# Pooled attention and a cosine-gated MLP on one core: another queue and another type for batch 0's loads

## The chip, the core and the metric

The kernel runs on one core of a Trainium2 chip. A core has a matrix engine (TensorE, "PE" in the profile, with its weight loads listed apart as "PEld"), a vector engine (VectorE, "DVE"), an activation engine (ScalarE, "ACT"), a general engine (GpSimd, "POOL") and SyncE ("SP"), which here only issues transfers. Sixteen DMA engines move data between the memory (HBM) and the on-chip memory (SBUF). Matrix products land in a small accumulator memory (PSUM) of eight banks; here they are three pairs (`banks`) and two single ones (`obanks`). An instruction waits at the head of its engine's queue until what it reads is there, and everything behind it on that engine waits with it.

The metric is the device time of one execution in microseconds (us); lower is better.

## The reference

Attention over keys and values that were averaged over groups of 8 positions, and then a two-layer network with the gate h · cos(h):

```python
B, H, S, D = 8, 8, 576, 64
k_p = k.reshape(B, H, 72, 8, D).mean(axis=3)
v_p = v.reshape(B, H, 72, 8, D).mean(axis=3)
attn = softmax(q @ k_p.T / sqrt(D))           # per batch and head, 576 x 72
x = (attn @ v_p), heads side by side          # 4608 tokens x 512
h = x @ w_in                                  # 512 -> 2048
out = (h * cos(h)) @ w_out                    # 2048 -> 512
```

All inputs and the output are fp32 in HBM; q, k and v are 9.4 MB each, the two weights 4.2 MB each.

## The kernel before

The 4608 tokens are cut into 9 tiles of 512. The loop over the tiles (t) does for each: the up projection into the eight pairs of hidden chunks (`up_mm`, L297), the gate (`up_g`: the cosine on ScalarE, L304, the product on VectorE, L307), and the down projection (`down_mm`, L310), between whose matmuls the attention of the next batch (b = t + 1) is woven by hand: `fill` holds pairs of "after so many matmuls" and "do this". The order of every engine's instructions is that of the program; nothing reorders them.

Batch 0 has nothing to be woven into. Its attention is the prologue, L334 to L423, and runs before the loop:

- `warm_up` (L392) issues matmuls on a constant tile, whose results nobody reads.
- q, k and v of one batch are staged in bf16 as `staged["q", 0]` and so on: 128 partitions, four pairs of heads (j = 0 to 3), 9 rows of 64 values each.
- `pool_k_mm` (L157) pools k by matmuls against a 0/1 matrix `groups`, which VectorE computes from iotas at the start (L361 to L365); `put_kk` (L132) copies the sums into `kk` in four copies. It is called for head pairs 0 and 1, and later for 2 and 3.
- `q_transpose_mm` (L192) transposes q by 18 matmuls against `identity`, in four groups, each followed by a copy into `qT` (L193).
- `scores` (L211, then an exponential on ScalarE, L218) works on one *unit*: 256 queries of four heads. Batch 0 has units 0 to 3 and a rest of 64 queries, which is done in the loop.
- `pool_v_mm` (L165) pools v by 18 matmuls of 256 columns into the two banks of a pair, and one VectorE copy (L167) puts the sums into `vz[0]`, whose other columns were filled with a constant before.
- `sums_first` (L266, then on ScalarE a logarithm, L270, and an exponential, L271) gives the inverse of a unit's softmax sums; `values_then` (L280) multiplies with v, and VectorE writes the product with the inverse into `xT` (L282), which the up projection reads. Units 0 and 1 give the first half of xT's four rows of chunks (ki 0 and 1), units 2 and 3 the second half. At the end of the prologue, the ki 0 and 1 part of the first two up projections is issued.

Batch 0's loads. The first half of k (head pairs 0 and 1) is loaded by SyncE in fp32 into the still unused `g_sb`, and ScalarE casts it into the staging tile (L342, L343). The others are casting transfers, fp32 in HBM to bf16 in SBUF, issued by GpSimd (`load_even`, L84): first half of q, second half of k, second half of q, all of v. Behind them on GpSimd's queue stand, in order: the identity (two instructions), w_in parts 0, 1 and 2 (`load_w_in`, L112), batch 1's k, the first half of its q, w_in part 3, the second half of its q, w_out part 0 (`load_w_out`, L117), batch 1's v, three fills of constant tiles, and w_out parts 1, 2 and 3. Eight casting transfers can be outstanding: from the ninth on, each issue waits until the one eight places before it has landed. In tile 0, the down projection goes through w_out's parts in order; part 1 is read from the ninth matmul on.

Of the kernel before, what the change touches and what calls it, by code (L numbers as in the profile page):

```python
# [9 lines left out]
FP32 = mybir.dt.float32  # L10
# [4 lines left out]
POOL = 8  # L15
# [4 lines left out]
def kernel(  # L20
# [42 lines left out]
    xT = wpool.tile([128, KCH, n_tokens], BF16, name="xT")  # L63
    g_sb = wpool.tile([128, FFCH, TILE], BF16, name="g_sb")
# [58 lines left out]
    half = (slice(0, 64), slice(64, 128))  # L123

    def v_part(b):
        return vz[b % 2][:, :, 0:4:3, :]

    def put_kk(b, ps, pj0, pj1, copy):
        dst = kk[b % 2].rearrange("p (j a) n -> p j a n", a=2)
        for a in range(2):  # L130
            for r in range(2):
                copy(out=dst[half[r], pj0:pj1, a, 0:Sp], in_=ps[half[a]])  # L132

    def pool_add(b, which):

# [14 lines left out]
    def pool_k_mm(b, bank, pj0, pj1):  # L150

        kb = staged["k", b]
        ps = bank[:, 0:(pj1 - pj0) * Sp].rearrange("p (j n) -> p j n", n=Sp)
        for pj in range(pj0, pj1):
            for t in range(ROW):
                for rows in half:
                    nc.tensor.matmul(ps[rows, pj - pj0, :], lhsT=kb[rows, pj, t, :], rhs=groups[rows, t, :],  # L157
                                     start=(t == 0), stop=(t == ROW - 1))
        return lambda copy: put_kk(b, ps, pj0, pj1, copy)

    def pool_v_mm(b, pair):
        vb = staged["v", b]
        for t in range(ROW):
            for hp, rows in enumerate(half):
                nc.tensor.matmul(pair[:Sp, hp, 0:KCH * D], lhsT=groups[rows, t, :], rhs=vb[rows, :, t, :],  # L165
                                 start=(t == 0), stop=(t == ROW - 1))
        nc.vector.tensor_copy(out=v_part(b).rearrange("p j a d -> p a j d"),  # L167
                              in_=pair[:Sp, :, 0:KCH * D].rearrange("p a (j d) -> p a j d", j=KCH))
# [31 lines left out]
    def scores(b, u, pair):  # L200
        scores_mm(b, u, pair)
        scores_exp(b, u, pair)
# [57 lines left out]
    def sums_first(b, u, cs):  # L260

        (c0, n), (h0, nh) = u
        ex = att["ex", b, u]
        for i in range(nh):
            hp = i % 2
            nc.tensor.matmul(cs[hp * 64:hp * 64 + 64, (i // 2) * n:(i // 2 + 1) * n], lhsT=ones[:Sp, :],  # L266
                             rhs=ex[:, ex_col(u, i):ex_col(u, i) + n])
        w = nh * n // 2
        lnc, inv = inverse_tile(w)
        nc.scalar.activation(out=lnc, in_=cs[:, 0:w], func=ACTF.Ln)  # L270
        nc.scalar.activation(out=inv, in_=lnc, func=ACTF.Exp, scale=-1.0)  # L271
        att["inv", b, u] = inv

    def values_then(b, u, ao):

        (c0, n), (h0, nh) = u
        ex = att.pop(("ex", b, u))
        for i in range(nh):
            pj, hp = divmod(h0 + i, 2)
            nc.tensor.matmul(ao[hp * 64:hp * 64 + 64, (i // 2) * n:(i // 2 + 1) * n],  # L280
                             lhsT=vz[b % 2][:, pj, 3 * hp, :], rhs=ex[:, ex_col(u, i):ex_col(u, i) + n])
        nc.vector.tensor_mul(out=x_out(b, u, slice(0, 128)), in0=cols(ao, u), in1=cols(att.pop(("inv", b, u)), u))  # L282
# [55 lines left out]

    kv_even_tiles(0)
    q_tile(0)  # L340
    k_first = g_sb.rearrange("p f n -> p (f n)").bitcast(FP32)[:, 0:2 * ROW * D]
    nc.sync.dma_start(out=k_first.rearrange("p (j n) -> p j n", j=2), in_=even_view(k, 0, 0, 2))  # L342
    nc.scalar.copy(out=staged["k", 0][:, 0:2].rearrange("p j t d -> p (j t d)"), in_=k_first)  # L343

    row_of = consts.tile([128, ROW], FP32, name="row_of")
    for rows in half:
# [2 lines left out]
    first_of = consts.tile([128, Sp], FP32, name="first_of")  # L349
    nc.gpsimd.iota(first_of, pattern=[[POOL, Sp]], base=0, channel_multiplier=0,  # L350
                   allow_small_or_imprecise_dtypes=True)
    load_even(staged["q", 0], 0, q, 0, 2)
    load_even(staged["k", 0], 0, k, 2, 4)
    load_even(staged["q", 0], 0, q, 2, 4)
    load_even(staged["v", 0], 0, v)
    identity = consts.tile([128, 128], BF16, name="identity")
    make_identity(nc, identity)
    dist = consts.tile([128, ROW, Sp], FP32, name="dist")
    sign = consts.tile([128, ROW, Sp], FP32, name="sign")
    groups = consts.tile([128, ROW, Sp], BF16, name="groups")  # L360
# [2 lines left out]
    nc.vector.scalar_tensor_tensor(out=sign, in0=dist, scalar=1.0 - POOL, in1=dist, op0=ADD,  # L363
                                   op1=mybir.AluOpType.mult)
    nc.vector.tensor_scalar(out=groups, in0=sign, scalar1=0.0, scalar2=None, op0=mybir.AluOpType.is_le)  # L365
    nc.vector.memset(vz[0], float(POOL))
    ones = consts.tile([128, D], BF16, name="ones")
    nc.vector.memset(ones, float(POOL))
    gate = consts.tile([1, 1], BF16, name="gate")
# [2 lines left out]

    kv_even_tiles(1)
    q_tile(1)
    for cg in range(3):
        load_w_in(cg)
    load_even(staged["k", 1], 1, k)
    load_even(staged["q", 1], 1, q, 0, 2)
# [1 line left out]
    load_even(staged["q", 1], 1, q, 2, 4)  # L380
    load_w_out(0)
    load_even(staged["v", 1], 1, v)
    nc.gpsimd.memset(vz[1], float(POOL))
    for i in range(2):
        nc.gpsimd.memset(kp2[i], 0.0)
    for cg in range(1, 4):
# [7 lines left out]
    vec, act = nc.vector.tensor_copy, nc.scalar.copy  # L394
    us = BY_HEADS

    warm_up(10, obanks[0])
    pool_k_mm(0, obanks[1], 0, 2)(vec)
    warm_up(2, banks[1][:, 0, :])
    puts = q_transpose_mm(0, banks[2][:, 0, :], 0, 5), q_transpose_mm(0, obanks[0], 5, 9)  # L400
    puts[0](vec)
    puts[1](act)
    warm_up(2, banks[1][:, 0, :])
    scores(0, us[0], banks[0])
    scores(0, us[1], banks[1])
    pool_k_mm(0, obanks[1], 2, 4)(vec)
    sums_first(0, us[0], banks[0][:, 0, :])
    for put in (q_transpose_mm(0, banks[2][:, 0, :], 9, 14), q_transpose_mm(0, obanks[0], 14, 18)):
        put(vec)
    sums_first(0, us[1], obanks[1])  # L410
    warm_up(2, banks[1][:, 0, :])
    scores(0, us[2], banks[0])
    scores(0, us[3], banks[2])
    pool_v_mm(0, banks[1])
    sums_first(0, us[2], obanks[0])
    values_then(0, us[0], obanks[1])
    values_then(0, us[1], banks[1][:, 0, :])
    sums_first(0, us[3], banks[2][:, 0, :])
# [6 lines left out]
    for t in range(NT):  # L425
        b = t + 1
# [108 lines left out]
```

## Time and profile before

| | us |
|---|---|
| runs | 302.17, 302.63, 302.64; median 302.63 |
| the profiled execution's span, first to last instruction | 301.4 |
| TensorE busy in the span | 293.9 (97%) |
| ScalarE, VectorE, GpSimd busy | 205.7, 170.8, 130.4 |
| first half of k (SyncE, fp32): issued, landed | 0.75, 4.4 |
| v of batch 0 (GpSimd, casting): issued, landed | 3.85, 14.5 |
| second pair of scores on TensorE | 13.07 to 13.70 |
| first up projection matmul (L297) | 18.38 |
| first down projection matmul (L310) | 34.62 |
| last matmul's end | 298 |

How to read it: the span is that of one execution that was recorded instruction by instruction; the runs' times also hold what lies before the first and behind the last instruction. "Busy" counts the time in which an engine worked on an instruction, its idle time is put down to what ended it. The chain of waits is followed back from the last instruction, at each step to what released it, so that its pieces add up to the span. A transfer's landing is the moment at which its completion is seen, reckoned from its issue. The table's times of single instructions are those of the timeline; its landings are issue plus "issue to landing" in the list of DMA issues, or the start of what waited for them.

### The profile page before, as it was taken

What the parts mean: (1) busy time and instruction counts of PE and PEld (TensorE: products, weight loads), DVE (VectorE), ACT (ScalarE), POOL (GpSimd) and SP (SyncE); (2) the same over time, 40 slices, a digit from 0 to 9 for tenths busy, and PEclk for the clock granted to TensorE, in tenths of its full rate; (3) what the DMA queues carried; (4) which work ended last, traced back from release to release, by engine and by line L of the source; (5) the groups of instructions that cost most, each with busy time, mean ns of one, the idle gap of its engine ahead of it and who ended that gap; (6) DMA issues with size and microseconds to landing.
All of it is one profiled execution on the core that took longest, in us unless ns stands there. A gap on an engine that the chain in (4) does not pass through costs nothing.

```text
span 301.4 us, 4625 instructions
## 1 busy us (share of the span) xinstructions
PE 293.9 (97%) x1816; PEld 143.2 (48%) x1816; DVE 170.8 (57%) x212; ACT 205.7 (68%) x254; POOL 130.4 (43%) x93
## 2 busy tenths in 40 slices
PE   8789999999999999999999999999999999999995
PEld 3445544445544454445444544455444544444444
DVE  5448637465467446754666556654775477425712
ACT  3786798469876987688778886789668966605500
POOL 8463016984983398239913990389300000000000
PEclk9999999999999999999999999999999999999999
DMA  7999999639526961697079617791811130131023
GB/s 152 197 207 206 206 205 195 141 55 176 117 60 124 167 127 29 146 158 140 6 170 143 129 36 171 94 174 39 141 32 35 37 70 0 37 70 35 0 67 75
DMA packets 44165, 32.91 MB, mean 109 GB/s; under 512 B 22128, under 2 KB 39408, under 8 KB 44144
## 3 DMA queue, kind: packets, MB, share of 16 engines
q0 software_dynamic: 19744, 18.07, 38.3%
q1 hardware_dynamic: 24160, 14.42, 20.5%
q8 instruction: 14, 0.23, 0.3%
q10 hardware_dynamic: 240, 0.13, 0.2%
q14 instruction: 7, 0.06, 0.1%
HBM read 36.70 MB, written 9.44 MB: 153 GB/s over the span
## 4 chain that ended last, share of the span: by engine, by line
PE 93%; DMA 4%; POOL 1%; DVE 1%; issue 0%; POOLq 0%; DVEq 0%
PE bank L297 41%; PE obank L310 41%; PE bank L241 5%; DMA kv_st<-in_v_dram 4%; PE bank L211 3%; PE bank L328 1%; PE bank L165 1%; POOL q_b L84 1%; PE obank L157 0%; PE obank L280 0%; PE obank L192 0%; DVE xT L282 0%; DVE vz L167 0%; POOL kv_st L84 0%; DVE o_sb L316 0%
## 5 line engine op out<-in xcount | busy, mean ns | idle before, releaser
L310 PE MATMUL obank<-w_out_sb,g_sb 128*128 128x512 bf16 x560 | 131.4, 379 | 0.0
L297 PE MATMUL bank<-xT,w_in_sb 128*128 128x512 bf16 x576 | 126.6, 379 | 0.0
L304 ACT ACTIVATE cos<-bank,half_pi 128x1024 f32<-128x1024 f32 x72 | 79.3, 1113 | 59.5 <-PE bank L297 59.5
L307 DVE TENSOR_TENSOR g_sb<-bank,cos 128x1024 bf16<-128x1024 f32 x72 | 87.3, 1223 | 43.0 <-ACT cos L304 42.9
L297 PEld LDWEIGHTS <-w_in_sb 128*128 128x128 bf16 x576 | 56.1, 98 | 67.6 <-issue 1.6
L310 PEld LDWEIGHTS <-g_sb 128*128 128x128 bf16 x560 | 52.8, 98 | 56.5 <-issue 2.0
L252 DVE TENSOR_TENSOR xT<-bank,inv 64x512 bf16<-64x512 f32 (+1 forms) x72 | 45.3, 629 | 40.8 <-ACT inv L248 40.1
L141 POOL TENSOR_TENSOR kv_st<-kv_st 72x2048 f32<-72x2048 bf16 x12 | 48.7, 4058 | 33.9 <-DMA kv_st<-in_k_dram 33.9
L247 ACT ACTIVATE lnc<-bank 64x512 f32<-64x512 f32 (+1 forms) x72 | 39.2, 544 | 3.1 <-PE bank L241 1.7
L316 DVE COPY o_sb<-obank 128x512 f32<-128x512 f32 x35 | 23.6, 689 | 30.9 <-PE obank L310 30.5
L218 ACT ACTIVATE ex<-bank 72x1024 bf16<-72x1024 f32 (+1 forms) x40 | 35.0, 929 | 8.5 <-PE bank L211 8.4
L142 POOL TENSOR_TENSOR kv_st<-kv_st 72x1024 f32<-72x1024 f32 x12 | 28.2, 2349 | 1.0
L248 ACT ACTIVATE inv<-lnc 128x512 f32<-128x512 f32 (+1 forms) x36 | 21.0, 583 | 1.1
L241 PE MATMUL bank<-ex,vz 72*128 72x256 bf16 (+1 forms) x176 | 20.0, 243 | 0.0
L241 PEld LDWEIGHTS <-vz 72*128 72x128 bf16 x176 | 13.6, 97 | 9.6 <-DVE xT L252 0.5
L145 POOL TENSOR_TENSOR kp<-kv_st 72x512 bf16<-72x512 f32 x12 | 14.9, 1263 | 0.5
L211 PE MATMUL bank<-qT,kk 64*72 64x256 bf16 (+1 forms) x192 | 13.2, 252 | 0.0
L211 PEld LDWEIGHTS <-kk 64*72 64x72 bf16 x192 | 7.4, 109 | 9.9 <-issue 7.2
L285 ACT ACT_TABLE_LOAD x9 | 11.5, 1283 | 0.9 <-PEq L519 0.7
L499 POOL COPY gate<-kk 1x1 bf16<-1x1 bf16 x5 | 0.9, 179 | 25.7 <-DMA kk<-kp 25.7
L288 ACT ACT_TABLE_LOAD x9 | 11.5, 1283 | 0.2
L103 POOL DMA_DIRECT2D kv_st<-in_v_dram x6 | 5.0, 841 | 8.8 <-PE bank L165 8.8
(55 smaller groups left out, 93.1 us busy)
## 6 DMA issues: line engine op xcount, KB each, us to landing
out_dram<-o_sb SPq DMA_DIRECT2D x70, 128.0 KB, 2.4
kv_st<-in_v_dram POOLq DMA_DIRECT2D x8, 576.0 KB, 13.7
kv_st<-in_k_dram POOLq DMA_DIRECT2D x7, 576.0 KB, 7.6
q_b<-in_q_dram POOLq DMA_DIRECT2D x6, 576.0 KB, 9.9
w_in_sb<-in_moe_w_in_dram POOLq DMA_DIRECT2D x4, 512.0 KB, 14.5
w_out_sb<-in_moe_w_out_dram POOLq DMA_DIRECT2D x4, 512.0 KB, 18.1
q_b<-in_q_dram POOLq DMA_DIRECT2D x4, 288.0 KB, 13.0
g_sb<-in_k_dram SPq DMA_DIRECT2D x1, 576.0 KB, 3.7
```

The source lines that it names most:

```text
L141: add(out=s, in0=x[:, :, 0:4, :], in1=x[:, :, 4:8, :], op=ADD)
L142: add(out=s[:, :, 0:2, :], in0=s[:, :, 0:2, :], in1=s[:, :, 2:4, :], op=ADD)
L211: nc.tensor.matmul(pair[:Sp, bank, c:c + n].rearrange("p (g n) -> p g n", n=64), lhsT=kk[b % 2][half[r], h0 + i, 0:Sp], rhs=att["qT", b][h ...
L218: nc.scalar.activation(out=ex[:, 0:nh * n].rearrange("p (a n) -> p a n", a=2), in_=pair[:Sp, :, 0:nh * n // 2], func=ACTF.Exp, scale=scale ...
L241: nc.tensor.matmul(pair[:, hp, (i // 2) * n:(i // 2 + 1) * n], lhsT=vz[b % 2][:, pj, 2 * hp:2 * hp + 2, :].rearrange("p a d -> p (a d)"), ...
L247: nc.scalar.activation(out=lnc[half[1 - hp]], in_=pair[half[1 - hp], hp, 0:w], func=ACTF.Ln)
L252: nc.vector.tensor_mul(out=x_out(b, u, half[hp]), in0=cols(pair[half[hp], hp, :], u), in1=cols(inv[half[1 - hp]], u))
L297: nc.tensor.matmul(h[:, j, :], lhsT=w_in_sb[fc // 4][:, ki, (fc % 4) * 128:(fc % 4 + 1) * 128], rhs=xT[:, ki, t * TILE:(t + 1) * TILE], st ...
L304: nc.scalar.activation(out=cos, in_=h, func=ACTF.Sin, bias=half_pi[:, :1])
L307: nc.vector.tensor_mul(out=g_sb[:, 2 * fp:2 * fp + 2, :], in0=h, in1=cos)
L310: nc.tensor.matmul(o, lhsT=g_sb[:, fc, ms * 128:(ms + 1) * 128], rhs=w_out_sb[fc // 4][:, fc % 4, :], start=(fc == 0), stop=(fc == FFCH - 1))
L316: nc.vector.tensor_copy(out=o[:, 0:n], in_=ps)
```

## The change

All of batch 0's q, k and v go over SyncE's queue in fp32, in six transfers of two head pairs each, in the order in which they are used: k, q, k, q, v, v. The first three land in `g_sb`, the other three in the last columns of `xT`, which later batches fill. Twelve casts (one head pair each, 128x576, `cast_first`) put them into the staging tiles in bf16: two on ScalarE, five on VectorE, five on GpSimd. GpSimd has no more loads of batch 0; its queue issues w_in part 0 behind its cast of v's first head pair, and the other loads behind its cast of v's last one. The constant fill of both `vz` moves to GpSimd's start. The prologue's own steps change as well: the last of the four first kk copies is ScalarE's, v is pooled and copied in two halves, with a cast between them on VectorE, the sums of units 2 and 3 follow the values of the units before them, and there are three fewer warm-up matmuls.

```diff
@@ put_kk @@
-                copy(out=dst[half[r], pj0:pj1, a, 0:Sp], in_=ps[half[a]])
+                put = copy[2 * a + r] if isinstance(copy, tuple) else copy
+                put(out=dst[half[r], pj0:pj1, a, 0:Sp], in_=ps[half[a]])
...
@@ pool_v_mm @@
-    def pool_v_mm(b, pair):
+    def pool_v_mm(b, pair, j0=0, j1=KCH):
         vb = staged["v", b]
+        n = (j1 - j0) * D
...
-                nc.tensor.matmul(pair[:Sp, hp, 0:KCH * D], lhsT=groups[rows, t, :], rhs=vb[rows, :, t, :],
+                nc.tensor.matmul(pair[:Sp, hp, 0:n], lhsT=groups[rows, t, :], rhs=vb[rows, j0:j1, t, :],
...
@@ the prologue @@
-    k_first = g_sb.rearrange("p f n -> p (f n)").bitcast(FP32)[:, 0:2 * ROW * D]
-    nc.sync.dma_start(out=k_first.rearrange("p (j n) -> p j n", j=2), in_=even_view(k, 0, 0, 2))
-    nc.scalar.copy(out=staged["k", 0][:, 0:2].rearrange("p j t d -> p (j t d)"), in_=k_first)
+    RAW = 2 * ROW * D
+    homes = [g_sb.rearrange("p f n -> p (f n)").bitcast(FP32)[:, i * RAW:(i + 1) * RAW] for i in range(3)]
+    homes += [xT[:, i, n_tokens - 2 * RAW:].bitcast(FP32) for i in range(3)]
+    raw = {}
+    for (w, src, j0), home in zip((("k", k, 0), ("q", q, 0), ("k", k, 2), ("q", q, 2), ("v", v, 0), ("v", v, 2)), homes):
+        raw[w, j0] = home.rearrange("p (j n) -> p j n", j=2)
+        nc.sync.dma_start(out=raw[w, j0], in_=even_view(src, 0, j0, j0 + 2))
+
+    def cast_first(w, j, copy):
+        copy(out=staged[w, 0][:, j].rearrange("p t d -> p (t d)"), in_=raw[w, j // 2 * 2][:, j % 2])
...
-    load_even(staged["q", 0], 0, q, 0, 2)
-    load_even(staged["k", 0], 0, k, 2, 4)
-    load_even(staged["q", 0], 0, q, 2, 4)
-    load_even(staged["v", 0], 0, v)
     identity = consts.tile([128, 128], BF16, name="identity")
     make_identity(nc, identity)
+    for i in range(2):
+        nc.gpsimd.memset(vz[i], float(POOL))
...
-    nc.vector.memset(vz[0], float(POOL))
...
-    for cg in range(3):
+    cast_first("k", 0, act)
+    cast_first("k", 1, vec)
+    cast_first("q", 0, pool)
+    cast_first("q", 1, act)
+    cast_first("k", 2, pool)
+    cast_first("q", 2, pool)
+    cast_first("v", 0, pool)
+    load_w_in(0)
+    cast_first("v", 3, pool)
+    for cg in range(1, 3):
         load_w_in(cg)
...
-    nc.gpsimd.memset(vz[1], float(POOL))
...
-    warm_up(10, obanks[0])
-    pool_k_mm(0, obanks[1], 0, 2)(vec)
-    warm_up(2, banks[1][:, 0, :])
+    warm_up(8, obanks[0])
+    pool_k_mm(0, obanks[1], 0, 2)((vec, vec, vec, act))
+    warm_up(1, banks[1][:, 0, :])
     puts = q_transpose_mm(0, banks[2][:, 0, :], 0, 5), q_transpose_mm(0, obanks[0], 5, 9)
     puts[0](vec)
     puts[1](act)
+    cast_first("k", 3, vec)
     warm_up(2, banks[1][:, 0, :])
     scores(0, us[0], banks[0])
     scores(0, us[1], banks[1])
+    cast_first("q", 3, vec)
     pool_k_mm(0, obanks[1], 2, 4)(vec)
...
     warm_up(2, banks[1][:, 0, :])
+    cast_first("v", 1, vec)
     scores(0, us[2], banks[0])
     scores(0, us[3], banks[2])
-    pool_v_mm(0, banks[1])
-    sums_first(0, us[2], obanks[0])
+    pool_v_mm(0, banks[1], 0, 2)
+    cast_first("v", 2, vec)
+    pool_v_mm(0, banks[1], 2, 4)
     values_then(0, us[0], obanks[1])
     values_then(0, us[1], banks[1][:, 0, :])
+    sums_first(0, us[2], obanks[0])
+    values_then(0, us[2], obanks[1])
     sums_first(0, us[3], banks[2][:, 0, :])
-    values_then(0, us[2], obanks[1])
     values_then(0, us[3], obanks[0])
```

More of the change, by code (lines that the diff above doesn't have):

```diff
@@ L159, in pool_k_mm @@
         return lambda copy: put_kk(b, ps, pj0, pj1, copy)
-    def pool_v_mm(b, pair):
+    def pool_v_mm(b, pair, j0=0, j1=KCH):
         vb = staged["v", b]
+        n = (j1 - j0) * D
         for t in range(ROW):
             for hp, rows in enumerate(half):
-                nc.tensor.matmul(pair[:Sp, hp, 0:KCH * D], lhsT=groups[rows, t, :], rhs=vb[rows, :, t, :],
+                nc.tensor.matmul(pair[:Sp, hp, 0:n], lhsT=groups[rows, t, :], rhs=vb[rows, j0:j1, t, :],
                                  start=(t == 0), stop=(t == ROW - 1))
-        nc.vector.tensor_copy(out=v_part(b).rearrange("p j a d -> p a j d"),
-                              in_=pair[:Sp, :, 0:KCH * D].rearrange("p a (j d) -> p a j d", j=KCH))
+        nc.vector.tensor_copy(out=v_part(b)[:, j0:j1].rearrange("p j a d -> p a j d"),
+                              in_=pair[:Sp, :, 0:n].rearrange("p a (j d) -> p a j d", d=D))
     def k_transpose(b):
@@ L374 @@
     q_tile(1)
-    for cg in range(3):
+    vec, act, pool = nc.vector.tensor_copy, nc.scalar.copy, nc.gpsimd.tensor_copy
+    cast_first("k", 0, act)
[8 more added lines that the diff above has]
+    for cg in range(1, 3):
         load_w_in(cg)
@@ L392, in warm_up @@
             nc.tensor.matmul(bank, lhsT=warm[:, 0:128], rhs=warm)
-    vec, act = nc.vector.tensor_copy, nc.scalar.copy
     us = BY_HEADS
-    warm_up(10, obanks[0])
-    pool_k_mm(0, obanks[1], 0, 2)(vec)
-    warm_up(2, banks[1][:, 0, :])
+    warm_up(8, obanks[0])
+    pool_k_mm(0, obanks[1], 0, 2)((vec, vec, vec, act))
+    warm_up(1, banks[1][:, 0, :])
     puts = q_transpose_mm(0, banks[2][:, 0, :], 0, 5), q_transpose_mm(0, obanks[0], 5, 9)
```

## The prediction

> **What bounds the kernel now.** First the busy shares on the page: TensorE is busy 97% of the span. So only TensorE's idle time can be won, and all of it lies in the first 18.4 us. Then the chain of waits in order of time, over the first 60 us:
>
> ```profile
> 3.85 10.62 DMA kv_st<-in_v_dram
> 14.51 0.72 PE bank L165 x10
> ...
> 15.78 0.70 DVE vz L167
> ...
> 17.04 0.70 DVE xT L282
> ...
> 17.78 0.63 PE obank L280 x8
> 18.41 8.80 PE bank L297 x40
> ```
>
> The load of batch 0's v is the wait that ends last. It lands at 14.5; L165 pools it, L167 copies it, L280 and L282 give xT, and at 18.4 the up projection (L297) starts. From there to the end the chain is TensorE alone: a shift that reaches this stage reaches the end in full.
>
> Next the DMA stretches. Columns: the stretch, its length, busy times by engine, clock, DMA share, GB/s.
>
> ```profile
> 3.00:3.50 0.50, 0.50 (x2) 0.15 (x1) 0.47 (x2) 0.00 (x0) 0.50 (x2) 1.00 1.04 410
> 14.00:43.00 29.00, 27.58 (x270) 14.68 (x270) 16.83 (x23) 23.59 (x33) 8.84 (x11) 1.00 1.23 206
> ```
>
> SyncE's one fp32 load runs at 410 GB/s. GpSimd's casting loads are counted in bf16: 206 GB/s written is 412 GB/s of fp32 read, so both kinds move the same data in the same time. And this stream never pauses from 5 to 43 us. How near TensorE runs to it is told by the issue of w_out part 1, the issue-to-landing time of that issue, and its first user:
>
> ```profile
> 20.69 0.75 POOL L117 DMA_DIRECT2D w_out_sb<-in_moe_w_out_dram  x1
> ```
> ```profile
> w_out_sb<-in_moe_w_out_dram POOLq DMA_DIRECT2D x1, 512.0 KB, 17.5
> ```
> ```profile
> 38.60 0.81 PE L310 MATMUL obank<-w_out_sb,g_sb 128*128 128x512 bf16 x3
> ```
>
> It lands at 20.69 + 17.5 = 38.2 and is read at 38.6: 0.4 us to spare. By the same sum, parts 2 and 3 land at 40.7 and 43.3 and are read at about 41.3 and 43.9 (0.6 each); w_in part 0 lands at 16.95, read at 18.4 (1.4); batch 1's v has 1.5, w_in part 3 1.7, the rest 1.9 or more. So there are two bounds: the chain through v, and 0.4 us behind it the weight stream. A gain above 0.4 us needs both to come earlier.
>
> **The change, step by step.** *Loads.* Six fp32 loads of 0.59 MB go out on SyncE from 0.75 on (0.46 us an issue, done by 3.6; its next work is at 46 us). k's first half lands at 4.4 as now; each further one costs 0.59/0.41 = 1.44: q 5.85, k 7.3, q 8.7, v 10.15, v 11.6. v's last half is 2.9 earlier than now.
>
> *Casts.* ACT: the row 128x1152 fp32 to bf16 takes 1.15, the 128x512 copy 0.59, so 576 columns about 0.66. VectorE: L365, fp32 to bf16 in SBUF, 0.50 for 648 columns, so 0.45 (bounds 0.36, half L361's two-input rate, and 0.75, all of it). GpSimd has no such row: a memset of 1024 columns takes 0.97, which gives 0.55; the two-input add L142 gives 2349/1024 x 576 = 1.3; the nearest, one input and two-byte output, is the affine select (128 columns, 0.29), so 0.7. All three are below the 1.44 spacing of the landings, so GpSimd keeps up.
>
> *Pass to the second scores.* k cast by ACT and VectorE 4.44-5.1 (now 5.6); pooling from 5.35 (now 5.85); four kk copies of 0.31 end 7.65 to 8.0 (now 8.46), one on ACT. q's transposes wait for GpSimd's cast (5.9-6.6) and end 7.6; qT copies end 8.2 and 8.6 (now 9.17, 9.49). The first scores move from 9.2 to 8.4, the exps to 9.1-11.0. Second pooling of k 9.2-10.0, kk copies to 11.3, qT to 12.1, second scores 12.2-12.8 (now 13.07-13.7): 0.9 won. VectorE's casts of k, q and v (0.45 each) lie in its gaps up to there; at 0.75 each they still do. Warm-ups fall from 16 to 13 and filled idle time; vz's fill (0.91, VectorE) goes to GpSimd, which is idle before 5.9.
>
> *v in halves.* Two poolings of 18 matmuls, paced by their weight loads (18 in 0.91), so 0.9 each where one took 1.17; two copies of 0.37 for one of 0.69. VectorE's cast of v's third part stands behind the first copy, and TensorE's second pooling behind that cast: 12.8-13.7 pool, 13.8-14.2 copy, 14.2-14.65 cast, 14.7-15.65 pool, to 16.15 copy. Values of units 0 and 1 then end at 16.05 and 16.55, their xT at 16.85 and 17.5: the up projection's first data is 0.8 earlier than now (18.32). But the sums of units 2 and 3 now follow the values. ACT, free at 15.35, starts L270 for unit 2 only at 16.95 (now 16.11); four activations of 0.63 follow, and unit 3's xT ends at 20.25 (now 19.6). TensorE starts L297 after the last values at 18.1, runs 8 matmuls (1.75) to 19.85 and waits for unit 3 until 20.3; now it is there at 20.15. So on this chain: +0.15, bounds -0.5 and +0.9 (the casts' ends; one more hop between engines at each of the six hand-overs, 0.06 each).
>
> *The weight stream.* w_in part 0 now stands behind GpSimd's cast of v: issue at 10.15 + 0.05 + 0.7 = 10.9 (bounds 10.6, 11.8), now 5.15. What an issue on an empty stream costs is seen at 94.83 us, where batch 4's loads are issued:
>
> ```profile
> 94.50:96.00 1.50, 1.50 (x9) 0.69 (x7) 1.00 (x2) 0.89 (x2) 1.35 (x3) 1.00 0.00 0
> 96.00:96.50 0.50, 0.50 (x4) 0.20 (x2) 0.50 (x1) 0.50 (x1) 0.50 (x2) 1.00 0.84 21
> 96.50:97.00 0.50, 0.50 (x4) 0.21 (x3) 0.03 (x1) 0.50 (x1) 0.50 (x1) 1.00 0.54 32
> 97.00:97.50 0.50, 0.50 (x4) 0.27 (x3) 0.47 (x1) 0.00 (x0) 0.28 (x1) 1.00 0.53 61
> 97.50:98.00 0.50, 0.50 (x4) 0.21 (x3) 0.50 (x1) 0.39 (x1) 0.00 (x0) 1.00 0.81 119
> 98.00:98.50 0.50, 0.50 (x5) 0.20 (x3) 0.25 (x1) 0.50 (x1) 0.00 (x0) 1.00 0.90 150
> ```
>
> Nothing flows for 1.3 us and the ramp loses (185+174+145+87+56)/206 x 0.5 = 1.57 from 96.0: the stream counts as full from 2.75 us after the issue (2.8 at 64.70; 3.3 for the first one, at 1.42; low bound 1.3, no ramp). So 13.65, while SyncE's data end near 11: the DMA engines idle 2.7 us, which they do not now. From part 0 to w_out part 1 there are 4 x 0.524 + 3 x 0.59 + 2 x 0.524 = 4.92 MB, 23.9 us at 206; a landing trails the bytes moved by 0.35 to 0.43 MB now, 1.9 us. Sum: 13.65 + 23.9 + 1.9 = 39.45, 1.25 after now's 38.2. Bounds: issue 10.6 + 1.3 gives -0.5, issue 11.8 + 3.3 gives +2.7. w_in part 0 lands near 17.7, before it is needed; the slacks of 1.4 and more also hold. At w_out part 1, TensorE arrives at 38.75 and waits 0.7.
>
> **Sum.** 0.15 + 0.7 = +0.85. The profiled span is 301.4, 1.2 below the runs' median of 302.63; that rest does not change. Predicted: 302.63 + 0.85 = 303.5.
>
> The Trainium skill (DMA: Bandwidth & Descriptors, Specifications) puts the HBM limit of one core at about 358 GB/s. No row here agrees: 410 for SyncE's load, 412 for the casting stream; by its figure each load would take 1.65, v's first half would land 0.8 later, and the sum, an estimate, would be +1.7.
>
> **The rivals.** (A) The forecast: a wait at w_out part 1 takes the place of the wait for v. For it: the 0.4 us, and two ramps alike. Against: the ramps seen are of 72-partition loads.
> (B) The ramp hides. With w_in part 0 on 128 partitions the stream is full soon after its first bytes, at 12.5; w_out part 1 lands at 38.3 and only the chain counts: +0.15, 302.8.
> (C) Faster: v early decides. If the stream is full by 11.9 (low bound), w_out part 1 lands 0.5 earlier, and if unit 3's xT comes by 19.3, which needs the 0.9 won at the second scores to pass through the late sums, TensorE gains 0.9: 301.7. Decides: w_out part 1 before 37.7. Against: GpSimd's issue behind the cast.
> (D) VectorE's casts hold GpSimd. v's two casts (12.1, 14.2) fall on GpSimd's cast and its issues of w_in 1 and after. If each holds it 0.45, and its own casts take 1.3 and not 0.7, the stream is 1.2 to 1.5 later still: about 304.8. For: GpSimd's issue beside L361 took 0.88, others 0.70. The Trainium skill (SBUF — State Buffer, SBUF: two separate sides) says that a VectorE fp32 copy within SBUF shuts GpSimd out, descriptors too; no run here shows it yet.
>
> **How the numbers follow.** About 0.2% (0.6 us) is what a measurement of this kernel can tell from no change. A 0.5, spread over +0.3 to +1.5: 0.43 slower, 0.07 same. B 0.25, same. C 0.09, faster. D 0.16, slower. Together faster 0.09, same 0.32, slower 0.59. The range takes A, B and most of D, and from C's side the chain's low bound: 302.2 to 305.0; the forecast's own is 302.9 to 304.2.
>
> **What would show it.** v's pooling starting near 12.8; w_in part 0 issued near 10.9, its bytes from 12.2; DMA idle around 12; w_out part 1 landing near 39.5 with TensorE waiting before it; unit 3's xT near 20.2. Wrong if w_out part 1 lands before 38.6, or if the up projection waits for w_in part 0.

## The result: slower, at the place that was named and by three times as much

| | before | changed |
|---|---|---|
| median of the runs, us (lowest to highest, 4 runs each) | 302.63 (302.17–302.75) | 305.24 (304.51–306.22) |
| ratio of the runs, 95% interval | | 1.0096 [1.0078, 1.0113] |
| span of the profiled execution | 301.4 | 304.0 (the longest; the others 302.4, 302.9, 303.3) |
| time outside the span (before: in its later executions, 1.73 to 1.86) | 1.8 | 2.15 |
| v of batch 0 seen as landed | 14.5 | 11.17 (first half) |
| w_in part 0 issued | 5.15 | 11.84 |
| first up projection matmul | 18.38 | 17.67 |
| w_out part 1 landed, first read | 38.2, 38.60 | 41.2, 41.23 |

The time rose by 2.6 us (0.96%) where +0.85 was forecast; 305.24 lies above the upper end of the range, 305.0. Ratios, here and below, are of fast executions alone; the one slow execution (308.23, over 1.5% above the fastest of its kernel, a later version) is left out of its ratio.

First the chain of waits of the changed kernel, 0 to 60 us, which answers to the chain shown of before. Columns: start, length, what.

```profile
2.77 8.40 DMA xT<-in_v_dram
11.17 0.05 issue
11.23 0.67 POOL kv_st L352
11.89 0.89 POOL w_in_sb L112
12.78 0.72 POOL kv_st L352
13.50 8.63 DMA w_in_sb<-in_moe_w_in_dram
22.13 0.29 issue
22.41 18.77 DMA w_out_sb<-in_moe_w_out_dram
41.19 0.04 issue
41.23 0.81 PE obank L312 x3
```

Before, the chain left the loads at 14.5 and was TensorE alone from 18.4 on. Now it stays with transfers up to 41.2: v lands, GpSimd casts it (L352), only then issues w_in part 0 (L112), casts again, issues the rest, and the weights arrive late one after the other. The line of w_out part 1's first reader on TensorE's timeline ends with the idle time ahead of it:

```profile
41.23 0.81 PE L312 MATMUL obank<-w_out_sb,g_sb 128*128 128x512 bf16 x3 [1.42 <-DMA w_out_sb<-in_moe_w_out_dram]
```

It starts 2.63 later than before's 38.60, the next tile's up projection 2.62 later (56.78 for 54.16 in the chains), and the last matmul ends 2.6 later: all of the span's loss arises ahead of this line. Span minus the start of this reader is 262.8 in both profiles (301.4 − 38.60, 304.0 − 41.23).

Then the stretches of half a microsecond (stretch, length, busy times by engine, clock, DMA share, GB/s), and the one of 14 to 43 that was shown of before:

```profile
10.50:11.00 0.50, 0.23 (x4) 0.23 (x5) 0.47 (x3) 0.50 (x1) 0.22 (x1) 1.00 1.04 397
...
12.50:13.00 0.50, 0.50 (x9) 0.29 (x8) 0.50 (x1) 0.47 (x2) 0.50 (x2) 1.00 0.00 0
13.00:13.50 0.50, 0.47 (x16) 0.41 (x16) 0.04 (x1) 0.50 (x2) 0.50 (x1) 1.00 0.02 4
13.50:14.00 0.50, 0.28 (x12) 0.13 (x6) 0.08 (x1) 0.50 (x1) 0.50 (x2) 1.00 0.70 45
14.00:14.50 0.50, 0.00 (x0) 0.00 (x0) 0.50 (x2) 0.50 (x2) 0.50 (x2) 1.00 0.81 104
14.50:15.00 0.50, 0.24 (x8) 0.24 (x10) 0.21 (x1) 0.50 (x1) 0.50 (x1) 1.00 1.12 172
15.00:15.50 0.50, 0.50 (x20) 0.41 (x16) 0.00 (x0) 0.13 (x1) 0.50 (x2) 1.00 1.22 201
...
17.00:17.50 0.50, 0.48 (x10) 0.26 (x6) 0.23 (x1) 0.47 (x2) 0.50 (x2) 1.00 0.92 96
17.50:18.00 0.50, 0.50 (x5) 0.21 (x3) 0.00 (x0) 0.47 (x2) 0.50 (x2) 1.00 0.82 102
...
20.00:20.50 0.50, 0.49 (x3) 0.25 (x3) 0.00 (x0) 0.50 (x1) 0.50 (x2) 1.00 1.23 201
```
```profile
14.00:43.00 29.00, 25.08 (x251) 13.07 (x255) 17.24 (x24) 20.25 (x28) 11.96 (x16) 1.00 1.19 195
```

SyncE's data end at 11.1, the weights' first bytes come at 13.5, and the rate climbs to 201 by 15.0. Then it falls to about 100 once more (16.5 to 18) and is full for good only from 20: two ramps where the prediction had one. Before, the stretch of 14 to 43 had 206 GB/s in the mean; now it has 195, and starts behind a gap.

### The profile page after: what moved, and what is told of

It is laid out like the page before. It is cut to its first block, busy times and chain, and to the rows that moved or that the text cites. A ratio compares the mean times of both kernels' runs of the same rounds, so it can differ in the third digit from the quotient of the medians.

```text
span 304.0 us, 4642 instructions
## 1 busy us (share of the span) xinstructions
PE 291.4 (96%) x1798; PEld 142.3 (47%) x1831; DVE 173.1 (57%) x216; ACT 206.3 (68%) x256; POOL 133.0 (44%) x95
## 4 chain that ended last, share of the span: by engine, by line
PE 84%; DMA 12%; issue 1%; POOL 1%; ACT 1%; SPq 1%; DVE 0%
PE obank L312 39%; PE bank L299 36%; DMA w_out_sb<-in_moe_w_out_dram 6%; PE bank L243 5%; PE bank L213 3%; DMA w_in_sb<-in_moe_w_in_dram 3%; DMA xT<-in_v_dram 3%; PE bank L330 1%; ACT ex L220 1%; SPq L349 1%; POOL kv_st L352 0%; POOL w_in_sb L112 0%; DVE o_sb L318 0%
## 5 line engine op out<-in xcount | busy, mean ns | idle before, releaser
L312 PE MATMUL obank<-w_out_sb,g_sb 128*128 128x512 bf16 x542 | 129.0, 380 | 2.3 <-DMA w_out_sb<-in_moe_w_out_dram 1.4
L243 PEld LDWEIGHTS <-vz 72*128 72x128 bf16 x176 | 13.6, 97 | 9.6 <-DVE xT L254 0.5
```

What stands on the lines that cost most here:

```text
L243: nc.tensor.matmul(pair[:, hp, (i // 2) * n:(i // 2 + 1) * n], lhsT=vz[b % 2][:, pj, 2 * hp:2 * hp + 2, :].rearrange("p a d -> p (a d)"), ...
L312: nc.tensor.matmul(o, lhsT=g_sb[:, fc, ms * 128:(ms + 1) * 128], rhs=w_out_sb[fc // 4][:, fc % 4, :], start=(fc == 0), stop=(fc == FFCH - 1))
```

## The experiments

Each is the changed kernel with one edit, unless it says "before". A ratio is to executions of before taken beside the run; their medians were 302.11 to 302.31, with median spans of 300.3 to 300.5. Time outside the span is a run's time less its span.

### Is it the late stream?

**Before with the stream made late.** Nothing of the change but its late weights: a copy of one element on GpSimd, which waits for v, stands ahead of w_in's issues.

```diff
     q_tile(1)
+    landed = consts.tile([1, 1], BF16, name="landed")
+    nc.gpsimd.tensor_copy(out=landed, in_=staged["v", 0][0:1, 0, 0, 0:1])
     for cg in range(3):
         load_w_in(cg)
```

> The kernel before with one thing added: a one-element GpSimd copy of staged v of batch 0 ahead of the weights' issues, so that w_in part 0 is issued when v has landed (14.5 us instead of 5.15). No other part of the change is in it. Theory 1: the DMA engines run empty after v; the stream counts as full at 14.5 + 2.75 = 17.3 and w_out part 1 lands at 17.3 + 25.8 = 43.1, 4.9 later than before; TensorE also waits for w_in part 0, near 20.5. The end is 4 to 5 us later than before's, about 307. Rival (the late start is hidden by later slack, and the changed kernel's loss comes from its casts and sums): within 1 us of before, or no more than the 2 us that the wait for w_in part 0 costs.

Measured: 305.92 (305.44–306.21), ratio 1.0122 [1.0104, 1.014]; spans 303.6 to 304.4. From its chain of waits:

```profile
3.83 9.74 DMA kv_st<-in_v_dram
...
13.81 2.18 POOL w_in_sb L112 x3
...
22.99 18.48 DMA w_out_sb<-in_moe_w_out_dram
```

The late stream alone, with none of the casts and none of the reordering, costs 3.8, and at the same reader (41.51). Three of the four executions had a mean granted clock of 0.994 or below; the one at full clock has a span of 303.6. In the profile the half clock (18.7 to 22.1) lies ahead of the reader, which waits for its weights all the same. The cost is below the 4 to 5 expected for two reasons: v landed at 13.6 here, not at 14.5 as in the profile of before, so that w_in was issued 0.9 earlier than reckoned; and the stream, with its three issues in a row, was full 2.3 after the first of them and not 2.75 (13.76; its shortfall below 206 GB/s from 14.5 to 20 sums to 1.54).

**The issues moved ahead of GpSimd's casts.** w_in parts 0, 1 and 2 go out behind its casts of k, q and v's first part; v's last cast follows.

```diff
     cast_first("k", 2, pool)
+    load_w_in(0)
     cast_first("q", 2, pool)
+    load_w_in(1)
     cast_first("v", 0, pool)
-    load_w_in(0)
+    load_w_in(2)
     cast_first("v", 3, pool)
-    for cg in range(1, 3):
-        load_w_in(cg)
```

> The changed kernel with one thing moved: GpSimd issues w_in parts 0, 1 and 2 between its casts (behind the casts of k's third head pair, q's third and v's first) and not behind the cast of v's first head pair. Theory 1 (the weight stream starts too late, and the wait at w_out part 1 sets the end): part 0 is issued near 9.3 us, its bytes flow when SyncE's end near 11, w_out part 1 lands near 37.9 instead of 41.2, TensorE doesn't wait for it, and the span falls by 2.3 from the changed kernel's, to about 301.3 to 301.6. Rival (the prologue's own chain sets the end: casts, late sums of units 2 and 3): the end doesn't move by more than 0.3. In between would say that the loads of q and v are slowed by the weights beside them.

Measured: 303.74 (302.78–306.02), ratio 1.0056 [1.0031, 1.0082]. The profiled span is 300.9; its timeline shows w_in part 0's issue and w_out part 1's reader:

```profile
8.46 0.95 POOL L112 DMA_DIRECT2D w_in_sb<-in_moe_w_in_dram  x1
```
```profile
38.04 0.81 PE L312 MATMUL obank<-w_out_sb,g_sb 128*128 128x512 bf16 x3
```

The issue is 3.4 earlier, and no idle time stands at the reader any more. Spans at full granted clock are 300.6 to 301.2, against 302.4 to 304.0 of the changed kernel and 299.8 to 301.0 of before beside it. So the order of GpSimd's queue is the cause of most of the span's loss: the middle of the four spans at full clock is 300.85, the changed kernel's 303.1, before's 300.4. The median shows less of it: four of the eight executions had a mean granted clock of 0.994 or below, with spans of 302.0 (one 303.9); see the third group.

**One load fewer.** w_in part 3 isn't loaded; part 2 is used in its place, so 0.52 MB less stand ahead of w_out part 1.

```diff
+    w_in_sb[3] = w_in_sb[2]
...
-    load_w_in(3)
```

> The changed kernel without the load of w_in part 3; its hidden chunks are computed with part 2, so the output differs from the reference's. The stream before w_out part 1 is 0.52 MB shorter, 2.55 us at 206 GB/s; nothing else changes. Theory 1: w_out part 1 lands near 38.6, the wait of 1.4 us before it and that of 0.3 for w_in part 3 go, and the span falls by 1.7 to 2.3. Rival (the chain of the prologue): no change.

Measured: 303.73 (303.09–304.26), ratio 1.0043 [1.0025, 1.0061]; spans at full clock 300.9 to 301.3 (three of six executions; the others, at 0.994, 301.9 to 302.1). TensorE comes to the reader, L313 here, without a wait:

```profile
39.27 0.81 PE L313 MATMUL obank<-w_out_sb,g_sb 128*128 128x512 bf16 x3
```

This profile is one of the 0.994. The casts, their order and their waits are the changed kernel's; only 2.5 us of transfer (0.52 MB at 206 GB/s) are gone, and with them 2.0 of the 2.7 that the changed kernel's spans lie above before's. So about 0.7 is left for anything else on TensorE's path.

**The sums back ahead of the values.** Unit 2's sums between the two poolings of v, unit 3's behind the second, as near to the order before as the halves allow.

```diff
     pool_v_mm(0, banks[1], 0, 2)
+    sums_first(0, us[2], obanks[0])
     cast_first("v", 2, vec)
     pool_v_mm(0, banks[1], 2, 4)
+    sums_first(0, us[3], banks[2][:, 0, :])
     values_then(0, us[0], obanks[1])
     values_then(0, us[1], banks[1][:, 0, :])
-    sums_first(0, us[2], obanks[0])
     values_then(0, us[2], obanks[1])
-    sums_first(0, us[3], banks[2][:, 0, :])
     values_then(0, us[3], obanks[0])
```

> The changed kernel with the sums of unit 2 between the two poolings of v and those of unit 3 behind the second one, ahead of the values; the loads stay late. Theory 1: unit 3's xT comes near 18.9 instead of 19.95, TensorE no longer waits for it in the up projection (0.4 us), and all of that is given back at w_out part 1: the time is the changed kernel's within 0.3 us. Rival (the prologue's chain sets the end): 0.6 to 0.8 us faster than the changed kernel.

Measured: 305.5 (304.19–305.86), ratio 1.0102 [1.0075, 1.0129]: the changed kernel's time. TensorE no longer waits for unit 3's xT. It waits for w_in's parts instead (0.49 and 0.50) and at the same reader as long as before the edit:

```profile
40.90 0.81 PE L312 MATMUL obank<-w_out_sb,g_sb 128*128 128x512 bf16 x3 [1.40 <-DMA w_out_sb<-in_moe_w_out_dram]
```

With the stream late, the order of the sums is worth nothing.

### Where does the second fall come from?

**All three issues in a row**, v's last cast behind them. It tells whether the fall at 16.5 comes from the cast that stands between the issues of parts 0 and 1.

```diff
-    load_w_in(0)
-    cast_first("v", 3, pool)
-    for cg in range(1, 3):
+    for cg in range(3):
         load_w_in(cg)
+    cast_first("v", 3, pool)
```

> The changed kernel with GpSimd's cast of v's last head pair moved behind the issues of w_in parts 1 and 2, so that the three issues stand together as they do in the run where v's landing alone held them back. Theory 1a (the second fall of the stream, 96 to 158 GB/s between 16.5 and 19.5 us, comes from the 1.66 us between the first and the second issue: a second ramp): the fall goes, w_out part 1 lands near 40.1 instead of 41.2 and the span falls by 0.8 to 1.1; the second pooling of v waits for its last cast, issued 1.5 later, near 15.0 and costs 0.2 at most. Rival 1b (the fall comes from VectorE's copies and products at that time, or from the ring's start as such): no change in landing beyond 0.3, the time is the changed kernel's.

Measured: 305.52 (304.96–306.43), ratio 1.0111 [1.0088, 1.0134]. From its stretches of 1 us:

```profile
14.00:15.00 1.00, 0.12 (x5) 0.23 (x7) 0.31 (x1) 1.00 (x2) 1.00 (x2) 1.00 1.20 197
15.00:16.00 1.00, 0.91 (x22) 0.66 (x20) 0.39 (x1) 0.24 (x1) 1.00 (x2) 1.00 1.25 208
16.00:17.00 1.00, 0.85 (x11) 0.64 (x12) 0.98 (x3) 0.18 (x1) 1.00 (x3) 0.78 1.22 198
17.00:18.00 1.00, 1.00 (x12) 0.83 (x8) 0.34 (x1) 0.97 (x2) 1.00 (x2) 0.50 1.25 209
18.00:19.00 1.00, 1.00 (x6) 0.28 (x3) 0.69 (x1) 0.94 (x3) 1.00 (x2) 0.50 1.24 206
...
23.00:24.00 1.00, 1.00 (x5) 0.38 (x4) 0.00 (x0) 0.44 (x1) 0.14 (x1) 0.81 1.21 209
```

The fall is gone (197 to 209 throughout), and w_out part 1 lands at 39.1 (issued 20.94, 18.2 to landing), 2 earlier; 1.8 earlier than in the changed kernel's second profile below, where part 0 was issued at the same time (11.41, here 11.43). So the cast between the issues made it. The time didn't follow: v's last cast ended at 14.8 and TensorE idled 1.5 ahead of the second pooling (busy 0.12 of 14 to 15), and then the column ahead of the DMA share, the granted clock, reads 0.50. By the shares at both ends (0.78 in 16 to 17, 0.81 in 23 to 24) the half clock lasted from 16.6 to 23.4. TensorE came to the reader at 40.99, now by its own slowness. That is one of the two executions at 0.988; the other two, at 0.998, have spans of 302.8 and 302.9, and what sets these no profile shows.

**First loads in two halves each**, nine SyncE loads instead of six, to see whether smaller loads are seen as landed sooner.

```diff
-        nc.sync.dma_start(out=raw[w, j0], in_=even_view(src, 0, j0, j0 + 2))
+        for j in ((0, 1), (1, 2)) if (w, j0) in (("k", 0), ("q", 0), ("v", 0)) else ((0, 2),):
+            nc.sync.dma_start(out=raw[w, j0][:, j[0]:j[1]], in_=even_view(src, 0, j0 + j[0], j0 + j[1]))
```

> The changed kernel with three of SyncE's six loads (first halves of k, q and v) cut in two: nine loads, the same bytes. Theory 2 (a landing trails the bytes moved by about one transfer, 0.59 MB, which is why v's first half lands at 11.2 and not at 10.15): v's first head pair, now a transfer of 0.29 MB of its own, lands near 9.8, GpSimd issues w_in part 0 near 10.5 instead of 11.85, and the time falls by 0.9 to 1.3. Rival (a landing is late because the loads are slower than 410 GB/s): v's first head pair lands at 10.4 or later and the time falls by 0.7 at most. Beside it: the time outside the span is 2.15 in the changed kernel and 1.8 in the one before. Should it hang on which of the eight completion counters the last stores use, it is 1.8 here, since nine loads bring these back to the places of the kernel before; should it hang on the number of SyncE's loads, it is 2.15 or more.

Measured: 305.52 (305.25–305.66), ratio 1.0107 [1.0092, 1.0122]. Only k's first half gained (cast from 3.64 instead of 4.47). The cast of q's second head pair started at 7.74 (5.86 before the edit), k's second half at 9.16 (8.31), w_in part 0 went out at 12.12 (11.84). Cutting the loads made later ones later, and the expectation that smaller loads are seen sooner fell. SyncE issued k's second half at 2.60 (1.75 before the edit), as two more issues stood ahead of it; whether that is the whole reason isn't shown.

### Does a mended version beat the kernel before?

**Early issues and early sums together** (the edits of the second and the fourth run).

> The changed kernel with both edits: w_in parts 0 to 2 issued between GpSimd's casts, and the sums of units 2 and 3 ahead of the values. Theory 1: with the stream no longer late, the late xT of unit 3 is what TensorE waits for (1.9 us from 17.65 in the first of these runs' trace), and the sums now count, which they didn't alone: span 0.4 to 0.7 below that of the kernel with earlier w_in alone, about 300.3 where the clock stays full. Rival (the sums don't matter here either): the same span as with earlier w_in alone, 300.9.

Measured: 303.82 (302.13–308.23, 10 runs), ratio 1.0037 [1.0003, 1.0071]. At full clock the spans are 300.0 to 301.2, the up projection starts at 16.92, and w_out part 1, landed at 37.0, is read at 37.14 without a wait. But five of ten executions had a mean clock of 0.994 or less, with spans of 302.2 and more (the longest, 306.1, at 0.978).

**More warm-ups.** First with the nine loads as well, then with six loads: one warm-up more ahead of the first pooling of k, one ahead of q's first transposes, two ahead of k's second pooling, two between the poolings of v.

```diff
-    warm_up(8, obanks[0])
+    warm_up(9, obanks[0])
     pool_k_mm(0, obanks[1], 0, 2)((vec, vec, vec, act))
-    warm_up(1, banks[1][:, 0, :])
+    warm_up(2, banks[1][:, 0, :])
...
     cast_first("q", 3, vec)
+    warm_up(2, obanks[0])
     pool_k_mm(0, obanks[1], 2, 4)(vec)
...
     sums_first(0, us[2], obanks[0])
+    warm_up(2, obanks[1])
     cast_first("v", 2, vec)
```

> All of these: earlier w_in, sums ahead, nine loads, and six more warm-up matmuls in TensorE's waits (one before the first pooling, one behind it, two before the second pooling of k, two between the poolings of v). If theories 1 and 2 hold and the half-clock stretches that some of the runs with earlier w_in showed (mean clock 0.994, spans 1.1 us longer) come from TensorE's idle time, the clock is 1.0 in all runs, the span about 300.0 and the time 0.2 to 0.6 below the kernel before. If warm-ups don't hold the clock, runs at 0.994 remain.

> The changed kernel with the three w_in issues between GpSimd's casts, the sums between the two poolings of v, six loads as in the change, and six more warm-up matmuls (one ahead of the first pooling of k, one ahead of the first transposes, two ahead of the second pooling of k, two between the poolings of v). Theory (the loss of the change is the late stream, and what is left over after mending it is TensorE's idle time in the prologue, which costs clock later): no execution below a granted clock of 0.998, span 300.3 to 301.0, and with 2.15 outside the span 302.4 to 303.1, about the kernel before. Rival (the lower clock has nothing to do with TensorE's idle time): half of the executions at 0.994 and a span of 302, as without the added warm-ups, so a median near 303.8.

Measured: 304.16 (303.37–304.3), ratio 1.0054 [1.0038, 1.0071] with nine loads, where TensorE waited 1.56 for the cast of q's second head pair and the up projection started late (19.4); 303.06 (302.56–303.49, 12 runs), ratio 1.0022 [1.0012, 1.0033] with six. All 16 executions were at 0.998 or above: the theory on the clock held. The size didn't: spans of 300.8 to 301.7, as the four warm-ups in the middle stood on TensorE's path (up projection at 18.39 in that profile).

**The warm-ups where TensorE waited anyway**: one ahead of q's second transposes, three between v's first pooling and the sums of unit 2, instead of those four.

> The early w_in issues and the early sums with six more warm-ups, but the four of them that stood on TensorE's path now stand where it waited: one ahead of the second transposes of q, three behind the first pooling of v, ahead of the sums of unit 2. Theory (the lower clock follows TensorE's idle time in the prologue, and the six warm-ups before cost 0.7 because four stood on the path): granted clock 0.998 and above in all executions, up projection at 16.9 to 17.3, span 300.0 to 300.8. Outside the span 1.8 or 2.15, so 301.8 to 303.0. Rival (what is filled in elsewhere comes back as idle time behind it, and the clock falls): half of the executions at 0.994 with 302.

Measured: 302.47 (301.79–303.14, 12 runs) beside 302.11 of before, ratio 1.001 [0.9999, 1.0021]; all 12 at 0.998 or above, spans 300.0 to 301.3. From its chain:

```profile
19.95 17.69 DMA w_out_sb<-in_moe_w_out_dram
37.64 0.04 issue
37.68 0.81 PE obank L312 x3
```

This is the best version of the new loads, and it isn't faster than before: the up projection starts at 17.17, but w_out part 1 ends the chain, landing no earlier than it does in before's second profile below (37.56). GpSimd is busy from 8 to 20 us with casts and issues in turn, and the stream isn't full beside them:

```profile
13.00:15.00 2.00, 2.00 (x39) 1.08 (x33) 0.79 (x2) 2.00 (x4) 2.00 (x3) 1.00 1.12 164
15.00:17.00 2.00, 1.41 (x23) 1.02 (x20) 1.59 (x3) 1.91 (x4) 2.00 (x4) 1.00 1.18 186
```

### Two sizes that were still open

**Both kernels once more**, unchanged, for a second profile of each.

> The kernel before once more, for a second profile of it. Theory (its profiled execution was one of its long ones, because v landed late in it): a span of 300.0 to 300.9, v's pooling at 13.2 to 14.1 instead of 14.5, the first up projection at 17.0 to 17.9 instead of 18.4, and no wait for w_out part 1. Rival (the prologue is always as in that profile, and the difference arises later or outside): the up projection at 18.3 to 18.5 whatever the span.

> The changed kernel once more, for a profile that is not its longest execution. Theory (the late weight stream sets the end): the wait for w_out part 1 is there in this one too, its landing at 40.0 to 41.2, and span minus landing as in the first profile, 262.8 up to 0.3. Rival (the wait belongs to that long execution only): no wait ahead of w_out part 1's user, or one below 0.3, and a span of 302.4 to 303.3 all the same.

Before, from the timeline of TensorE:

```profile
13.79 1.17 PE L165 MATMUL bank<-kv_st,groups 64*72 64x256 bf16 x18 [0.22 <-DMA kv_st<-in_v_dram]
...
17.66 1.67 PE L297 MATMUL bank<-xT,w_in_sb 128*128 128x512 bf16 x7
...
37.88 0.81 PE L310 MATMUL obank<-w_out_sb,g_sb 128*128 128x512 bf16 x3
```

Span 300.7, time 302.47: v landed at 13.8, and TensorE waited 0.22 for it instead of the 0.8 that the first profile had between the second scores and the pooling. The first profile was one of before's long executions; 23 others beside this one have a median span of 300.3. w_out part 1 landed at 19.96 + 17.6 = 37.56, 0.3 ahead of its reader, so the two bounds lie as close together here. The second profile of the changed kernel has span 303.8: v at 10.75, w_in part 0 issued at 11.41, TensorE waits 0.92 for w_in part 3 (0.34 in the first profile) and 1.39 for w_out part 1:

```profile
40.95 0.81 PE L312 MATMUL obank<-w_out_sb,g_sb 128*128 128x512 bf16 x3 [1.39 <-DMA w_out_sb<-in_moe_w_out_dram]
```

The wait belongs to the kernel, not to one long execution.

**What the time outside the span hangs on.** It was 2.1 to 2.2 in the changed kernel and five of its variants, all with six SyncE loads, and 1.75 to 1.9 in before, with one, and in the two runs with nine. Three runs test the number of loads: before with five tiny loads of 32 KB more, and the two versions with warm-ups with three tiny loads more.

```diff
+    for i in range(5):
+        nc.sync.dma_start(out=xT[:, 3, n_tokens - 128 * (i + 1):n_tokens - 128 * i].bitcast(FP32), in_=q[0, i, 0:128, :])
```

> The kernel before with five tiny SyncE loads of 32 KB behind its one fp32 load, so that SyncE issues six loads ahead of its stores, as the changed kernel does, while all else stays. If the time outside the span hangs on the place of the stores behind the loads, it is 2.15 instead of 1.8, and the time 0.35 above the kernel before, plus up to 0.4 from the 164 KB that stand ahead of the casting stream: 302.9 to 303.4. If it belongs to the size or the type of the changed kernel's loads, it stays at 1.8: 302.6 to 303.0.

> The same with three more SyncE loads of 32 KB behind the six, into columns of xT that nothing reads before they are written again; SyncE issues nine loads ahead of its stores, as in the kernel whose first loads were cut in two. If the time outside the span hangs on which place in a row of eight the last stores take, it is 1.8 instead of 2.15, with the same span up to 0.2 (98 KB are 0.24 us of the transfers' rate): 302.1 to 302.8, at or just below the kernel before. If it hangs on the six loads themselves, it stays at 2.15 or grows.

> The same with three tiny SyncE loads of 32 KB behind the six. The span as without them, up to 0.2; outside the span 1.8, if anything in the number of SyncE's loads plays a part there, so 301.8 to 302.6, at or below the kernel before; if the loads play no part, the same time as without them.

Measured: before with six loads 303.41 (302.8–303.9), ratio 1.003 [1.0019, 1.0041], outside the span 1.76 to 1.86; with nine loads 303.06, ratio 1.0019 [1.0009, 1.003], and 302.72, ratio 1.0018 [1.0006, 1.0031], both 1.76 to 1.84. But the versions with warm-ups and six loads have 1.75 to 1.86 as well. The number of loads doesn't decide it; the theory fell, and what does decide it stays open (no trace shows the eight places that two of the expectations speak of). The time of before with five tiny loads (+1.1 in the span) shows how little its prologue bears: 0.16 MB ahead of the casting stream.

## Why the prediction was right in kind and wrong in size

The forecast's mechanism, a wait at w_out part 1 in place of the wait for v, is what the trace shows and what the first three runs confirm. What was off is its size: +2.61 for +0.85, a miss of 1.76. Its pieces, worked out at the medians: span is time less what lies outside, 302.63 − 1.8 = 300.83 before and 305.24 − 2.15 = 303.09 changed; less 262.8, the reader of w_out part 1 starts at 38.03 and 40.29. The prediction had 38.6 and 39.45.

- **The weight stream, mis-sized by 0.84** (40.29 for 39.45; 1.75 and 1.5 in the two profiles). Two of its terms failed. *v's landing*: 11.17 and 10.75 for 10.15. The step "each further one costs 1.44" failed at one load: from the second landing to the third it took 2.45 and 2.0, and 1.4 to 1.5 at the other three steps (5.85, 8.3, 9.7, 11.17 in the first profile, 5.85, 7.9, 9.3, 10.75 in the second). The bytes came as reckoned (397 GB/s at 10.5), but from the third load on a landing is seen further behind the bytes moved than the 0.2 to 0.3 MB of the first two: 0.6 MB in the first profile, 0.4 in the second. Why, no run shows. *The stream counts as full 2.75 after the issue*: it was 3.6 (15.46 − 11.84), with the shortfall below 206 GB/s from 13.0 to 20.5 summed to 2.46 us; in the second profile 3.4. With the three issues in a row it was 2.5 (13.9 − 11.43). So one ramp cost no more than reckoned; what the term lacked is the second one, about 1 us, made by the cast between the issues. The rest of the sum held: 15.46 + 23.9 + 1.9 = 41.26, measured 41.19, which is beyond the upper bound that the prediction gave this landing (38.2 + 2.7 = 40.9). GpSimd's cast at 0.7, the least certain price, was 0.66, which was partly luck: the rows named beside it give 0.55 and 1.3, and 0.7 doesn't follow from them.
- **The time of before, mis-read by 0.57** (38.03 for 38.6). "That rest does not change" took the 1.2 between the profiled span and the median for something outside the span. It was 1.8 outside less a long execution in the profile. Every step was then measured from a v that landed late.
- **Outside the span, 0.35**, was not foreseen and isn't explained.

*The chain through the prologue*, forecast at +0.15, came out within 0.3 of it. The up projection started at 17.67 (forecast 18.1) and waited for unit 3's xT until 20.01 (forecast 20.3), where before stood at 20.15: −0.15. In the second profiles the wait ended at 19.59, where before stood at 17.66 + 1.77 = 19.43: +0.15. The second scores at 12.43 and v's pooling at 13.09 were forecast at 12.2 and 12.8; the late sums then did give back what was won, as reckoned.

*"The slacks of 1.4 and more also hold"* failed with the stream's size: 3 us of delay instead of 1.25 used up the 1.7 of w_in part 3.

*The rivals.* B (the ramp hides) is out: two ramps, nothing hidden. C is out in this kernel; the versions with early issues show the mechanism (up projection at 16.9 to 17.2), and that the other bound then takes it. D is partly real, in its mechanism and not in its place. From the timelines of the changed kernel:

```profile
2.40 1.83 POOL L364 MEMSET vz<- 72x1024 bf16 x2
3.20 1.38 DVE L372 TENSOR_SCALAR groups<-sign 128x648 bf16<-128x648 f32 x1
5.89 0.66 POOL L352 CAST q_b<-g_sb 128x576 bf16<-128x576 f32 x1 [1.67 <-DMA g_sb<-in_q_dram]
8.31 0.46 DVE L352 CAST kv_st<-g_sb 128x576 bf16<-128x576 f32 x1 [0.72 <-DMA g_sb<-in_k_dram]
8.34 0.95 POOL L352 CAST kv_st<-g_sb 128x576 bf16<-128x576 f32 x1 [1.79 <-DMA g_sb<-in_k_dram]
```

From the second profile, where GpSimd's cast of k began first, and from before:

```profile
7.89 0.67 POOL L352 CAST kv_st<-g_sb 128x576 bf16<-128x576 f32 x1 [1.31 <-DMA g_sb<-in_k_dram]
8.02 0.85 DVE L352 CAST kv_st<-g_sb 128x576 bf16<-128x576 f32 x1
```
```profile
3.21 0.50 DVE L365 TENSOR_SCALAR groups<-sign 128x648 bf16<-128x648 f32 x1
```

GpSimd's cast takes 0.66 alone and 0.95 behind VectorE's; VectorE's takes 0.46 alone and 0.85 behind GpSimd's, and its L372, 0.50 before (L365), takes 1.38 behind the fill that the change put on GpSimd. So each holds the other up, by 0.3 to 0.9, but not where D had it: the cast of v ahead of w_in part 0 took 0.67. That part's issue took 0.95, those behind it 0.72 to 0.81; how much of this is VectorE isn't shown. The prediction put the fill's move to GpSimd at nothing; the delay of L372 cost nothing here, as TensorE's first pooling of k started behind ScalarE's cast, which ended at 5.14. The Trainium skill (SBUF — State Buffer, SBUF: two separate sides) calls the port pair the two share an exclusive lock held for a whole instruction, by whichever starts first. The trace agrees, in both directions: 0.66 to 0.95, 0.46 to 0.85, 0.50 to 1.38. What each lost is 0.14 or 0.15 less than the time for which the other still ran (0.29 of 0.43, 0.39 of 0.54, 0.88 of 1.03).

## What to carry to other kernels

An engine's queue that casts and issues loads ties the loads to the data it casts: look at what stands behind the cast on that queue, not only at who reads the cast. A stream that ran without a pause was paid for twice when it was interrupted, with the idle time and with a second ramp for the gap between its issues. And one profile is one execution: take the spans of several runs before a remainder is put outside the span, and expect no more from moving one bound than its distance to the next, 0.3 us here.

## What the hardware showed that was not expected

- **TensorE's idle time in the prologue costs clock behind it.** With the stream mended, 4 of 8 and 5 of 10 executions ran below a mean clock of 0.995. So did 12 of the 22 of the late stream in before, one load fewer, early sums alone, issues together and nine loads; none of the changed kernel's five did, and 1 of 78 of before's. With six more warm-ups, which compute nothing, none of 52 did, also where the warm-ups only filled gaps. In the profiles the clock reads 0.50 for 3.4 us at a time (17.2 to 20.6 with one load fewer, 17.8 to 21.2 with nine loads, 18.7 to 22.1 with the late stream in before) or for 6.8 (16.6 to 23.4, issues together). The Trainium skill (TensorE: Matmul & The Clock Gate, What's actually happening) describes half rate decided in free-running windows of about 3.4 us by how busy TensorE was. The trace agrees with the half and with the length, once or twice 3.4. That the windows run free, which would make it some executions and not others, no run here shows.
- **From the third of several loads in flight on, a landing is seen late**: 0.4 to 0.6 MB behind the bytes moved, 0.2 to 0.3 for the first two. Cutting loads in two delayed later ones by 0.85 and 1.9.
- **The time outside the span isn't a constant of the kernel's shape**: 1.8 or 2.15 in variants that differ by a few warm-ups.
